# Sliding-window attention and a two-layer feed-forward in float32: value products by key block in array quarters, k and v in rings, whole scores in the opening, TensorE dummies and a new order

## The chip, the cores and the metric

The kernel runs on one core of one Trainium2 chip. The metric is the device time of one execution in microseconds (us); the median of the runs is given, and a profiled execution stands beside it.

## What is computed

Inputs are q, k and v of 8 batches, 8 heads, 576 positions and 64 columns, and the weights of a feed-forward network of 512 columns with 2048 hidden units. Positions see the 64 positions up to their own.

```
scores = q @ k.T / sqrt(64)                # where 0 <= i - j < 64, else -1e9
attn   = exp(scores - max) ; attn = attn / (sum + 1e-9)
x      = attn @ v, heads side by side       # 4608 x 512
h      = x @ w_in                           # 4608 x 2048
g      = max(h, 0) + alpha * min(h, 0)
out    = g @ w_out                          # 4608 x 512
```

The weights arrive as float64 bit patterns in int32 pairs and are made into floats on the chip.

## The kernel before, in words

The 4608 positions are 36 tiles of 128. A tile spans two query blocks of 64, each of which needs two key blocks of 64, so it needs three key blocks. The 8 heads are four pairs; two pairs lie above each other on the partitions (a "couple" of heads is the half of the partitions that a pair takes). For each tile t:

- `q_load`, `k_load` (three key blocks) and two `v_load` (two key blocks each) fetch into two buffers a name. Neighbouring tiles share a key block, which is fetched twice for k, and v is fetched twice over.
- `a_score` (line 433) writes the scores with products of 64x64 weights on 128 columns, in two PSUM banks, one for each half of the partitions. In the steady part both halves are written in one go, four quarters of the array side by side; in the opening tiles 0 to 2 (`WHOLE`) are too, tiles 3 to 8 one half at a time, with one bank each.
- `a_least` (444, VectorE) adds the mask and finds the maximum, `a_exp` (451, ACT) takes the exponential and its sum, `a_sum`, `a_inverse`, `a_scale` (462, 467, 473) divide.
- The weights of attention are turned: in the opening by TensorE (`a_turn`, 490) and a copy (`a_turned`, 495 or 497), later by VectorE's 32x32 transposes (`a_transpose`, 485).
- `a_value` (507) multiplies with v: 16 products with 128 rows (two key blocks) and 64 columns of weights, two halves of the array side by side, into one bank. `a_xh` (513, ACT) and `a_xl` (518, VectorE) split the result into a high and a low float32r part.

The feed-forward works on blocks of 2 or 3 tiles (`SIZES`), each in 16 cells of 128 hidden units. `m_hidden` (565) makes 12 products of high and low parts (high times high, low times high, high times low) into one of two PSUM buffers ("ph"); `m_slopes` (574, ACT), `m_larger` (580, VectorE), `m_high` (587, ACT) and `m_low` (594, POOL) make the activation and its two parts; `m_add` (608) makes three products for each tile into its output bank, two cells later (`LAG`).

float32 products are recorded twice each by the profile, float32r products once.

Weights come in 32 chunks (`raw`), and VectorE, ACT and POOL turn each into a high and a low part (lines 339 to 390: `two`, `man`, `exp`, `val`, then `win_h`, `win_l` or `wout_h`, `wout_l`). This and the attention of tiles 0 to 8 and the first three blocks of two tiles make the opening. Its order is written by a planner: `opening_graph` lists the operations with an engine, a cost and what they need; `list_schedule` walks through time and gives each engine, among what is ready and finds a buffer, the operation with the highest rank. The rank is the longest path to the end plus a number from `favour` (`TILE_FAVOUR`, `BLOCK_FAVOUR`, `KIND_FAVOUR`). PSUM has 8 banks in three pools: "po" 3, "psa" 3, "ph" 2. From tile 9 on, the order is written by hand: `eighth` cuts the attention of a tile into eight portions that are placed between cells; scores of tile t+1 and values of tile t-1 are in the last portion, next to each other.

Of the kernel before, what the change touches and what calls it, by code (L numbers as in the profile page):

```python
# [14 lines left out]
ALU = mybir.AluOpType  # L15
# [10 lines left out]
WHOLE = (0, 1, 2)  # L26
# [11 lines left out]
def opening_graph():  # L38
# [9 lines left out]
    def load(name, service, after=(), take=(), queue="SP"):  # L48
        op("i." + name, queue, 0.64, after, [take] * bool(take) + [("lane " + name, ["lane"])])
        op(name, "DMA", service, ["i." + name], free=["lane " + name])  # L50
# [6 lines left out]
    for t in range(EARLY + 1):  # L57
        done = [f"s.{t-2}.0", f"s.{t-2}.1"] if t > 1 else []
        load(f"q.{t}", 1.05, done, queue="ACT" if t == 0 else "SP")
        load(f"k.{t}", 1.6, done)  # L60
        for u in range(2):
            load(f"v.{t}.{u}", 1.05, [f"av.{t-2}"] if t > 1 else [])
    for c in range(2 * NCELL):
        load(f"raw.{c}", 2.0 if c % 2 else 2.2, take=(f"raw.{c}", ["raw"]))

    for t in attention:
        bank = ["po", "psa"] if t < 2 else ["psa"]
        score = [f"k.{t}", f"q.{t}"]
        score += ([f"s.{t-1}.0", f"s.{t-1}.1"] if t else []) + ([f"av.{t-2}"] if t > 1 else [])
        if t in WHOLE:  # L70
            op(f"s.{t}.0", "PE", 0.94, score, take=[(f"s.{t}.0", bank), (f"s.{t}.1", bank)])
            op(f"s.{t}.1", "PE", 0.0, [f"s.{t}.0"], done=0.0)
        for u in range(2):
            if t not in WHOLE:
                op(f"s.{t}.{u}", "PE", 0.87, score, take=(f"s.{t}.{u}", bank))
            for e in range(NH_PAIRS):
                g = u * NH_PAIRS + e
                op(f"le.{t}.{g}", "DVE", 0.21,
                   [f"s.{t}.{u}"] + ([f"tu.{t-2}.0", f"tu.{t-2}.1"] if t > 1 else []) + (["le.%d.0" % t] if g else []),
                   free=[f"s.{t}.{u}"] if e == NH_PAIRS - 1 else [], done=0.36)  # L80
                op(f"ex.{t}.{g}", "ACT", 0.39, [f"le.{t}.{g}"], done=0.6)
            op(f"sm.{t}.{u}", "ACT", 0.25, [f"ex.{t}.{u*NH_PAIRS+e}" for e in range(NH_PAIRS)], done=0.35)
# [3 lines left out]
            op(f"td.{t}.{u}", "ACT" if t > 1 else "DVE", 0.55 if t > 1 else 0.6,  # L86
               [f"tu.{t}.{u}"] + ([f"av.{t-2}"] if t > 1 else []), free=[f"tu.{t}.{u}"])
        op(f"av.{t}", "PE", 1.0, [f"td.{t}.0", f"td.{t}.1", f"v.{t}.0", f"v.{t}.1"]
           + ([f"h.{(t-RING)//2}.{last}"] if t >= RING else []), take=(f"av.{t}", bank))
        op(f"xh.{t}", "ACT", 0.5, [f"av.{t}"])  # L90
        op(f"xl.{t}", "DVE", 0.6, [f"xh.{t}"], free=[f"av.{t}"])

# [20 lines left out]
    for n in range(3):  # L113
        pair = [2 * n, 2 * n + 1]
        for f in range(NCELL):
            before = [f"h.{n}.{f-1}"] if f else [f"h.{n-2}.{last}"] if n > 1 else []
            op(f"h.{n}.{f}", "PE", 1.44, [f"lo.{2*f}"] + [f"xl.{t}" for t in pair] + before,
# [642 lines left out]
```

## Time and profile before

| | before |
|---|---|
| median of the runs | 934.62 us (934.35 to 934.86, 3 runs) |
| profiled execution | 934.54 us, its span 932.8 us |
| TensorE products busy | 912.3 us, 6601 records |
| VectorE, ACT, POOL busy | 438.0, 430.5, 348.1 us |
| moved by DMA | 69.78 MB, 75 GB/s on the mean; 254 GB/s in the first fortieth |
| loads, KB each, us to landing | q 256, 4.3; k 384, 4.7; v 256, 4.2; raw 512, 4.1 and 3.6 |

PE is TensorE's products, PEld its weight loads, DVE VectorE, ACT ScalarE, POOL GpSimd, SP the engine that issues most DMAs. A row of the windows has a stretch, its length, each engine's busy time with its count of instructions, the clock, the share of the DMA engines and what they moved. A row of the chain of waits has a start, a length, an engine, what it makes and its line. A row of the timeline has start, length, engine, line, operation, out<-in, shape and count, and in brackets the idle time before it with what ended it.

### The profile page before, as it was taken

To read this page: it belongs to the slowest core of one execution; us is meant where nothing else is said; L and a number is where in the kernel's file an instruction comes from. 1 tells how busy PE (TensorE), PEld (TensorE's weight loads), DVE (VectorE), ACT (ScalarE), POOL (GpSimd) and SP (SyncE) were. 2 spreads that over 40 slices of the span, in tenths; PEclk is the share of its full clock that TensorE was granted. 3 is DMA by queue.
4 is the path that set the end of the run, shared out by engine and by line. 5 is a ranking of instruction groups with operands and counts; after the bars stand their busy time and mean duration, and the time that the engine had idled before them with its cause. 6 is when DMAs were issued, how large, how long until landed. Compare 5 with 4: busy or idle time off the path is not lost.

```text
span 932.8 us, 17053 instructions
## 1 busy us (share of the span) xinstructions
PE 912.3 (98%) x6601; PEld 812.3 (87%) x6601; DVE 438.0 (47%) x1329; ACT 430.5 (46%) x1204; POOL 348.1 (37%) x330
## 2 busy tenths in 40 slices
PE   4899999999999999999999999999999999999998
PEld 3688889888988888888889889888888888889997
DVE  5798981224544444444444444444443443443111
ACT  5887884454444434434444444444443443432322
POOL 3889994224222233333222232332322222222221
PEclk9999999999999999999999999999999999999999
DMA  9775641111322112211122112222112212100000
GB/s 254 212 207 176 192 147 46 52 54 45 102 52 85 51 52 66 55 51 52 52 53 85 51 52 86 51 52 85 52 51 55 83 51 52 57 1 1 34 1 34
DMA packets 55216, 69.78 MB, mean 75 GB/s; under 512 B 3408, under 2 KB 48480, under 8 KB 55136
## 3 DMA queue, kind: packets, MB, share of 16 engines
q1 hardware_dynamic: 54832, 68.43, 26.0%
q8 instruction: 52, 0.85, 0.4%
q10 hardware_dynamic: 304, 0.27, 0.1%
q14 instruction: 28, 0.23, 0.1%
HBM read 59.25 MB, written 9.44 MB: 74 GB/s over the span
## 4 chain that ended last, share of the span: by engine, by line
PE 94%; DVE 2%; POOL 2%; ACT 1%; DMA 1%; issue 0%; POOLq 0%; DVEq 0%
PE h L565 43%; PE o L608 42%; PE s L433 4%; PE av L507 4%; PE t L490 1%; ACT w L451 1%; POOL val L375 1%; DMA q<-qT 1%; POOL w L473 0%; POOL gl L594 0%; POOL wout_l L390 0%; POOL win_l L390 0%; DVE exp L363 0%; DVE val L369 0%; DVE two L342 0%
## 5 line engine op out<-in xcount | busy, mean ns | idle before, releaser
L594 POOL TENSOR_TENSOR gl<-g,gh 128x384 fp32r<-128x384 f32 (+1 forms) x208 | 197.3, 948 | 548.9 <-ACT gh L587 543.3
L580 DVE SCALAR_TENSOR_TENSOR g<-h,s_sb,g 128x384 f32<-128x384 f32 (+1 forms) x208 | 122.0, 587 | 336.4 <-ACT g L574 333.6
L574 ACT ACTIVATE g<-h,sa_sb 128x384 f32<-128x384 f32 (+1 forms) x208 | 115.6, 556 | 262.7 <-PE h L565 258.4
L608 PE MATMUL o<-wout_h,gl 128*128 128x512 f32 x576 | 227.6, 395 | 1.2 <-POOL gl L594 1.2
L608 PE MATMUL o<-wout_l,gh 128*128 128x512 f32 x576 | 226.9, 394 | 0.0
L608 PE MATMUL o<-wout_h,gh 128*128 128x512 f32 x576 | 224.2, 389 | 0.0
L565 PE MATMUL h<-xh,win_h 128*128 128x384 f32 (+1 forms) x832 | 174.2, 331 | 0.4 <-DVE g L580 0.3
L565 PE MATMUL h<-xl,win_h 128*128 128x384 f32 (+1 forms) x832 | 168.8, 324 | 0.0
L565 PE MATMUL h<-xh,win_l 128*128 128x384 f32 (+1 forms) x832 | 167.8, 323 | 0.0
L587 ACT CAST gh<-g 128x384 fp32r<-128x384 f32 (+1 forms) x208 | 101.6, 489 | 124.4 <-DVE g L580 118.6
L565 PEld LDWEIGHTS h<-xh,win_h 128*128 128x128 f32 x832 | 141.3, 188 | 18.8 <-issue 1.2
L485 DVE STREAM_TRANSPOSE pt<-w 32x256 f32<-32x256 f32 x324 | 141.2, 436 | 5.5
L565 PEld LDWEIGHTS h<-xl,win_h 128*128 128x128 f32 x832 | 142.4, 188 | 0.1
L565 PEld LDWEIGHTS h<-xh,win_l 128*128 128x128 f32 x832 | 139.6, 188 | 0.0
L608 PEld LDWEIGHTS o<-wout_h,gh 128*128 128x128 f32 x576 | 108.1, 188 | 24.2
L451 ACT ACTIVATE w<-w,nm 128x128 f32<-128x128 f32 x288 | 113.1, 396 | 28.0 <-DVE nm L444 27.7
L608 PEld LDWEIGHTS o<-wout_h,gl 128*128 128x128 f32 x576 | 108.1, 188 | 18.5 <-POOL gl L594 1.8
L608 PEld LDWEIGHTS o<-wout_l,gh 128*128 128x128 f32 x576 | 108.3, 188 | 13.5
L444 DVE CUSTOM_DVE_ANT_0 w<-s,masks 128x128 f32<-128x128 f32 x288 | 71.1, 285 | 15.6 <-PE s L433 15.3
L473 POOL TENSOR_TENSOR w<-w,rc 128x1024 f32<-128x1024 f32 (+1 forms) x45 | 70.0, 1558 | 18.8 <-DVE rc L467 18.8
L518 DVE TENSOR_TENSOR xl<-av,xh 128x512 fp32r<-128x512 f32 x36 | 24.9, 691 | 99.6 <-ACT xh L513 99.5
L433 PEld LDWEIGHTS s<-k,q 64*64 64x64 f32 x1152 | 39.4, 142 | 24.0 <-PE o L608 9.6
(46 smaller groups left out, 535.1 us busy)
## 6 DMA issues: line engine op xcount, KB each, us to landing
v<-vN SPq DMA_DIRECT2D x72, 256.0 KB, 4.2
k<-kT SPq DMA_DIRECT2D x36, 384.0 KB, 4.7
out<-os SPq DMA_DIRECT2D x36, 256.0 KB, 2.3
q<-qT SPq DMA_DIRECT2D x35, 256.0 KB, 4.3
raw<-w_in SPq DMA_DIRECT2D x16, 512.0 KB, 4.1
raw<-w_out SPq DMA_DIRECT2D x16, 512.0 KB, 3.6
q<-qT ACTq DMA_DIRECT2D x1, 256.0 KB, 5.2
alpha_rows<-alpha ACTq DMA_DIRECT2D x1, 8.0 KB, 5.0
```

The lines of the kernel that those rows point to most:

```text
L433: nc.tensor.matmul(s[x][us, 2 * a + h], q[r, a, h, us], k[r, a, u:u + 2, h, :], start=True, stop=True)
L444: nc.vector.tensor_tensor_reduce(out=d["w"][:, g, :], in0=d["s"][u][:, e], in1=mask, op0=ALU.add, op1=ALU.min, scale=-SCALE, scalar=3.0e38 ...
L451: nc.scalar.activation(w, w, AF.Exp, scale=-1.0, bias=d["nm"][:, g:g + 1], accum_out=d["sm"][:, g:g + 1])
L473: nc.gpsimd.tensor_tensor(out=w, in0=w, in1=rc.unsqueeze(2).broadcast_to(list(w.shape)), op=ALU.mult)
L485: nc.vector.transpose(pt[ks, :, r], w[r, :, ks])
L507: nc.tensor.matmul(av[r, e, us], v[:, e, u, r], pt[:, g, us], start=True, stop=True)
L565: nc.tensor.matmul(ph[:, :nt], wt[:, c, fs], xt[:, c, xs], start=(k == 0), stop=(k == 3 * NP - 1))
L574: nc.scalar.activation(g, ph[:, :nt], AF.Copy, scale=sa_sb[:, f:f + 1])
L580: nc.vector.scalar_tensor_tensor(out=g, in0=ph[:, :nt], scalar=s_sb[:, f:f + 1], in1=g, op0=ALU.mult, op1=ALU.max)
L587: nc.scalar.copy(gh, gs[n, f])
L594: nc.gpsimd.tensor_tensor(out=gl, in0=g, in1=gh.bitcast(F32), op=ALU.subtract)
L608: nc.tensor.matmul(po[t], gt[:, ts], wt[:, f, :], start=(f == 0 and k == 0), stop=(f == NF - 1 and k == 2))
```

## The change

- **Values.** `a_value` takes each key block by itself: 32 products of 64x64 weights on 64 columns, four quarters of the array side by side, two of them (the index b) added up in PSUM. The two halves of the partitions go to two banks; outside the opening these are one "psa" and one "ph". High and low parts are then split by half: two `a_xh` and two `a_xl` for each tile, 256 columns each.
- **Rings.** k and v are const tiles of 7 key blocks (`KRING` = 3 tiles). Two tiles of three fetch only their two new key blocks; the third fetches three. v is one load for a tile.
- **Scores.** All tiles of the opening write both couples in one go. Tile 0 alone (`APART`) writes the two pair groups one after the other, and its q and k come in two loads each.
- **Layout.** The weights of attention lie as [pair group, key block, head, 64] so that the turned weights have each couple on its half of the partitions. `a_transpose` makes four transposes where it made three, two of them on half the columns; `a_scale` makes two calls of four heads in the steady part as well.
- **Dummies.** 60 products of the 128x128 identity with itself (`WARM`), at the lowest rank, in one "po" bank. The identity is now made before the masks.
- **First cells.** For the first three cells of each block (`FINE`) the three groups of products are operations of their own: high times high needs no low part. `m_add` starts with the high part.
- **Planner.** Other load costs, other favours with a third number for each kind, ties broken by index, and `MOVED`, a list of 13 copies given to VectorE (six `td`, seven `xh`); the other `td` go to ACT. The planner can also move `gl`, `pr`, `lo` and the sign of a chunk to VectorE; the list has none of these.

```diff
-WHOLE = (0, 1, 2)
+APART = (0,)
+WARM = 60
+FINE = 3
+KRING = 3
+MOVED = (
+    "td.0.0", "td.0.1", "td.4.0", "td.5.0", "td.5.1", "td.8.1", "xh.1.0", "xh.3.0", "xh.4.1", "xh.5.0",
+    "xh.5.1", "xh.6.0", "xh.7.0",
+)
...
+    for i in range(WARM):
+        op(f"wm.{i}", "PE", 1.2 if i == 0 else 0.25, [f"wm.{i-1}"] if i else [], take=("wm", ["po"]) if not i else (),
+           free=["wm"] if i == WARM - 1 else [])
...
+        values = ["po", "psa"] if t < 2 else ["psa", "ph"]
...
+    def k_load(t, a=None):
+        at = 2 * (t % KRING)
+        new = 1 if at else 0
+        part = slice(0, 2) if a is None else slice(a, a + 1)
+        from_ = kT[:, :, 2 * t + new:2 * t + 3].rearrange("(a x) d b h w -> (x d) a (b h w)", x=2)
+        nc.sync.dma_start(kring[:, part, at + new:at + 3].rearrange("p a b h w -> p a (b h w)"), from_[:, part])
+
+    def v_load(t):
+        at = 2 * (t % KRING)
+        new = 1 if at else 0
+        nc.sync.dma_start(vring[:, :, at + new:at + 3].rearrange("p a b d -> p a (b d)"),
+                          vN[:, :, 2 * t + new:2 * t + 3].rearrange("(a x) w b d -> (x w) a (b d)", x=2))
...
-        for e in range(NP):
+    def a_value(t, banks=("psa", "ph")):
+        pt, at = pts[t % 2], 2 * (t % KRING)
+        st[t]["av"] = av = [a_bank(f"av_{t}_{x}", from_) for x, from_ in enumerate(banks)]
+
+        for a in range(2):
             for u in range(2):
-                for h in range(2):
-                    r, us, g = slice(h * D, (h + 1) * D), slice(u * W, (u + 1) * W), e % 2 * NP + e // 2 * 2 + h
-                    nc.tensor.matmul(av[r, e, us], v[:, e, u, r], pt[:, g, us], start=True, stop=True)
+                for b in range(2):
+                    for h in range(2):
+                        for x in range(2):
+                            r, us, hs = slice(x * W, (x + 1) * W), slice(u * W, (u + 1) * W), slice(h * D, (h + 1) * D)
+                            nc.tensor.matmul(av[x][hs, a, us], vring[r, a, at + u + b, hs], pt[r, a, b, h, us],
+                                             start=b == 0, stop=b == 1)
...
-        for k, (gt, wt) in enumerate(((gl, wout_h), (gh, wout_l), (gh, wout_h))):
-            nc.tensor.matmul(po[t], gt[:, ts], wt[:, f, :],
+        for k in parts:
+            of_g, wt = (("gh", wout_h), ("gl", wout_h), ("gh", wout_l))[k]
+            nc.tensor.matmul(po[t], g[of_g][:, ts], wt[:, f, :],
                              start=(f == 0 and k == 0), stop=(f == NF - 1 and k == 2))
...
+    def warm(i):
+        if i == 0:
+            cv["warm"] = ps_o.tile([P, E], F32, tag="po", name="warm")
+        nc.tensor.matmul(cv["warm"][:, :P], ident, ident, start=True, stop=True)
```

More of the change, by code (lines that the diff above doesn't have):

```diff
@@ L58, in opening_graph @@
         done = [f"s.{t-2}.0", f"s.{t-2}.1"] if t > 1 else []
[L59 to L62, printed above, removed]
-    for c in range(2 * NCELL):
-        load(f"raw.{c}", 2.0 if c % 2 else 2.2, take=(f"raw.{c}", ["raw"]))
+        for a in range(2) if t in APART else ("",):
+            part = 0.5 if t in APART else 1.0
+            load(f"q.{t}" + f".{a}" * (a != ""), 0.8 * part, done, queue="ACT" if t == 0 else "SP")
+            load(f"k.{t}" + f".{a}" * (a != ""), (1.2 if t % KRING == 0 else 0.8) * part, done)
@@ L69, in opening_graph @@
[L69 to L72, printed above, removed]
-        for u in range(2):
[L74 to L77, printed above, removed]
+        before = ([f"s.{t-1}.0", f"s.{t-1}.1"] if t else []) + ([f"av.{t-2}"] if t > 1 else [])
@@ new lines, in opening_graph @@
+        for u in range(2):
+            loaded = [f"{x}.{t}.{u}" if t in APART else f"{x}.{t}" for x in "qk"]
+            banks = [(f"s.{t}.{x}" + ".1" * (u and t in APART), bank) for x in range(2)]
+            if t in APART:
+                op(f"s.{t}.{u}", "PE", 0.5, loaded + before + [f"s.{t}.0"] * u, take=banks)
+            elif u == 0:
+                op(f"s.{t}.0", "PE", 0.94, loaded + before, take=banks)
+            else:
+                op(f"s.{t}.1", "PE", 0.0, [f"s.{t}.0"], done=0.0)
@@ L280, in banded_attention_then_prelu_ffn @@
     ps_a = ctx.enter_context(tc.tile_pool(name="ps_a", bufs=3, space=PSUM))
+    ident = const.tile([P, P], F32, name="ident")
+    nc.gpsimd.memset(ident, 1.0)
+    nc.gpsimd.affine_select(out=ident, in_=ident, compare_op=ALU.is_equal, fill=0.0,
+                            base=0, pattern=[[-1, P]], channel_multiplier=1)
     masks = const.tile([P, 3, KW], F32, name="masks")
@@ L325, in banded_attention_then_prelu_ffn, with on, late_sign @@
     cv = {}
+    graph = opening_graph()
+    def on(name):
+        return {"POOL": nc.gpsimd, "DVE": nc.vector}[graph[name].engine if name in graph else "POOL"]
+    def late_sign(c):
+        return c % 2 == 1 and graph[f"lo.{c}"].engine == "DVE"
     def fetch(c):
@@ L346, in exponent @@
         two = cv[c]["two"]
-        nc.scalar.activation(two, two, AF.Relu, scale=8.0, bias=ebias if c % 2 else ebias20)
+        nc.scalar.activation(two, two, AF.Relu, scale=8.0, bias=ebias if c % 2 and not late_sign(c) else ebias20)
     def mask_mantissa(c):
@@ new lines, in of_x, with a_xh, a_xl @@
+    def of_x(t, of, x):
+        n, i = tiles[t]
+        return of.rearrange("p (a x) t -> p x a t", x=2)[:, x, :, (place[n] + i) * P:(place[n] + i + 1) * P]
+    def a_xh(t, x):
+        high, av = of_x(t, xh, x), st[t]["av"][x][:, :2]
+        if f"xh.{t}.{x}" in graph and graph[f"xh.{t}.{x}"].engine == "DVE":
+            nc.vector.tensor_copy(high, av)
+        else:
+            nc.scalar.copy(high, av)
+    def a_xl(t, x):
+        nc.vector.tensor_tensor(out=of_x(t, xl, x), in0=st[t]["av"][x][:, :2], in1=of_x(t, xh, x).bitcast(F32),
```

322 lines of the change are left out of this document (180 added, 142 removed).

## The prediction

> **What bounds the kernel now.** I read the page first, then the table of windows, then the chain of waits in three stretches, then single rows of the timeline.
>
> ```profile
> span 932.8 us, 17053 instructions
> PE 912.3 (98%) x6601; PEld 812.3 (87%) x6601; DVE 438.0 (47%) x1329; ACT 430.5 (46%) x1204; POOL 348.1 (37%) x330
> PE 94%; DVE 2%; POOL 2%; ACT 1%; DMA 1%; issue 0%; POOLq 0%; DVEq 0%
> ```
>
> TensorE is busy for 98% of the span and holds 94% of the chain that ended last. The other engines are below half on average, but the average hides the opening:
>
> ```profile
> core 0: us, PE busy (x) PEld busy (x) DVE busy (x) ACT busy (x) POOL busy (x), PEclk, DMA share, GB/s
> 0.00:10.00 10.00, 2.19 (x33) 1.76 (x33) 1.83 (x19) 2.36 (x6) 3.42 (x13) 1.00 0.87 214
> 10.00:20.00 10.00, 6.89 (x74) 5.45 (x75) 7.58 (x35) 7.93 (x32) 3.12 (x3) 1.00 1.10 293
> 20.00:30.00 10.00, 6.35 (x72) 4.63 (x70) 8.34 (x30) 7.05 (x27) 7.97 (x7) 1.00 0.96 267
> 30.00:40.00 10.00, 8.76 (x76) 7.42 (x74) 8.31 (x30) 8.71 (x29) 6.41 (x7) 1.00 0.70 202
> 60.00:80.00 20.00, 19.57 (x151) 16.89 (x150) 18.05 (x32) 15.40 (x33) 19.78 (x19) 1.00 0.52 157
> 100.00:120.00 20.00, 20.00 (x163) 17.51 (x163) 19.59 (x46) 17.34 (x45) 20.00 (x20) 1.00 0.60 191
> 200.00:900.00 700.00, 700.00 (x4944) 628.74 (x4943) 305.94 (x964) 287.75 (x823) 204.93 (x181) 1.00 0.20 55
> ```
>
> There are three stages. Until 30 us TensorE is busy for 2.19 + 6.89 + 6.35 = 15.4 us; half of the time it waits. From 60 us it is full, but up to 120 us (in these rows) so are POOL (19.78 and 20.00 of 20) and VectorE (18.05 and 19.59), which convert the weights. From 200 us TensorE alone is full. So work taken off TensorE after 60 us shortens the run directly, unless POOL holds it in the middle stage; before 33 us only the chain of waits counts.
>
> The chain of waits in the opening:
>
> ```profile
> 0.81 5.20 DMA q<-qT
> 6.06 2.05 PE s L433 x32
> 12.71 1.13 PE t L490 x4
> 14.70 1.10 PE t L490 x4
> 23.28 2.04 PE s L433 x30
> 28.76 1.55 PE av L507 x24
> 30.31 1.93 PE s L433 x22
> 89.56 1.02 PE s L433 x16
> ...
> 104.67 0.44 PE t L490 x4
> 110.79 1.02 PE s L433 x16
> 111.81 1.63 PE h L565 x12
> 114.81 1.44 PE h L565 x12
> ```
>
> and in the steady part:
>
> ```profile
> 610.11 1.03 PE s L433 x32
> 611.15 1.08 PE av L507 x32
> 612.23 2.28 PE h L565 x12
> 616.57 2.11 PE h L565 x12
> ```
>
> (Each float32 product stands twice in the records, so a tile's 16 score products are x32.) Two things are to be seen. All 32 records of a tile take 1.03 us where both couples run together; a half with one couple, 16 records, takes 1.02, as long for half the work. And the same pieces cost double at the start: 2.05 against 1.03 for scores, 1.13 against 0.44 for four transposes. TensorE runs at half speed until past 30 us, although the clock column prints 1.00 there. The first cell of the feed-forward part starts right behind:
>
> ```profile
> 32.86 0.74 PE L565 MATMUL h<-xh,win_h 128*128 128x256 f32 x4
> ```
>
> **The change part by part.** The profiled execution took 934.54 us for its span of 932.8, beside a median of 934.62 for the runs, so I sum against 934.5.
>
> **Scores of both couples at once.** Tiles 3 to 8 scored in halves. A half costs 1.02 and slows its neighbour by the switch of tile shape (1.63 against 1.44 for h: 0.2), 1.22 in all; two cost 2.44. A whole tile costs 1.03 + 0.2 = 1.23. That saves 1.2 per tile; tiles 4 to 8 lie where TensorE is nearly full, so 5 x 1.2 = **-6.0**. The price is that two PSUM banks are taken at one moment; a wait for that would show in front of the scores.
>
> **Value products in quarters.** 32 products of 64x64 on 64 columns replace 16 of 128x64 on 64 columns: 64 records instead of 32, but four side by side where there were two, so again 16 steps. The rows for one step:
>
> ```profile
> 586.92 1.10 PE L433 MATMUL s<-k,q 64*64 64x128 f32 x32
> 587.95 1.01 PEld L507 LDWEIGHTS av<-pt,v 128*64 128x64 f32 x32 [0.17 <-issue]
> 587.95 1.15 PE L507 MATMUL av<-pt,v 128*64 128x64 f32 x32
> 610.04 0.34 PE L433 MATMUL s<-k,q 64*64 64x128 f32 x4
> L433 PE MATMUL s<-k,q x1152: 269/269/473, 6.1 to 808.4; 64*64 64x128 f32 x192
> L507 PE MATMUL av<-pt,v x1152: 222/222/370, 15.7 to 853.7; 128*64 128x64 f32 x192
> issue: 5.7, 29
> ```
>
> Less the last product's own 0.22, 1.15 leaves 0.93 for 15 pair steps: 0.062 each for 64 columns. Scores leave 1.10 - 0.27 = 0.83 for 7 steps of four, 0.119 for 128 columns. Twice the columns, nearly twice the time, with two or four side by side: the step follows the columns. The first four scores of a tile lie within 0.34 us, where one alone lasts 0.27 or more, so issuing four takes hundredths. I therefore keep 0.062 and count **0**, with 0.119 (the score step) as the upper bound and nothing below zero, since the columns stay.
>
> **The border between scores and values.** Both now use the same quarters. The value weights waited 0.17 in the row above; in all 5.7 us over 29 waits, 0.20 each ("issue" on that line). If the quarters stay as they are, this wait goes. The bounds are 0 and 0.20; I take 0.13, because the next step would have taken 0.062 anyway. In the steady part 25 tiles (values 9 to 33) have scores directly ahead: 25 x 0.13 = **-3.3**.
>
> **The head: dummies, split loads, finer first cells.** The half-speed pieces on the chain shrink if the clock is up: scores 2.05 to 1.03 and 2.04 to 1.03, transposes 2.23 to 0.88, values and scores 1.55 and 1.93 to 0.8 and 1.03, together 5.0 less. But between them stands VectorE's queue (8.34 of 10 us busy from 20 to 30), so a part is only handed to it: I take half, -2.5. Tile 0's loads come in halves, so the first scores need half the bytes of the 5.20 us load; I take -0.5, because the dummies are in front of them: ten queued products of 128 columns at half speed (two records of 0.22 each) are 4.4 us, which begin only when POOL has made the identity that they multiply. The first three cells no longer wait for low parts, and k and v fetch a third less while the DMA is full (0.87 to 1.10 of share until 30 us): -1.5 together. Dummies that land behind real work: 60 x 2 x 0.119 = 14 us at full speed, and TensorE stands idle for 14.6 of the first 30, so nearly all fits; I add +0.8. Sum: **-3.7**. The bounds are -9 (VectorE's idle time from 10 to 40 us, 30 - 7.58 - 8.34 - 8.31 = 5.8, and 3 for an earlier start) and +7 (half of the dummies in the way, nothing gained). The sizes -0.5, -1.5 and +0.8 are choices inside these bounds.
>
> The Trainium skill, page "TensorE: Matmul & The Clock Gate", section "What's actually happening", says that the clock doubles after some 3.4 us of sustained matmuls and falls back after a window without any. The trace agrees in part: with 6.89 busy of 10 it stayed slow, and it rose only after the unbroken run from 28.76 on. By that rule the dummies raise it at 5 to 9 us.
>
> **At no cost.**
>
> ```profile
> L580 DVE SCALAR_TENSOR_TENSOR g<-h,s_sb,g 128x384 f32<-128x384 f32 (+1 forms) x208 | 122.0, 587 | 336.4 <-ACT g L574 333.6
> L574 ACT ACTIVATE g<-h,sa_sb 128x384 f32<-128x384 f32 (+1 forms) x208 | 115.6, 556 | 262.7 <-PE h L565 258.4
> L485 DVE STREAM_TRANSPOSE pt<-w 32x256 f32<-32x256 f32 x324 | 141.2, 436 | 5.5
> L518 DVE TENSOR_TENSOR xl<-av,xh 128x512 fp32r<-128x512 f32 x36 | 24.9, 691 | 99.6 <-ACT xh L513 99.5
> ```
>
> Each eviction of values (0.69 on VectorE) becomes two of half the columns, and a tile's 12 VectorE transposes of 0.44 become 16, half of them of half length: under 1 us per tile on engines that are busy for 306 and 288 of 700 us. POOL scales the same elements in two halves. One value bank now comes from the pair of buffers that h turns over. The next h then needs the previous cell's buffer back; between lie nine o products (in the chain from 612.23 + 2.28 to 616.57, 2.06), scores and values, 2.06 + 1.03 + 1.08 = 4.2 us, while slope and maximum take 0.56 + 0.59. Three microseconds of cover remain; gone, it would cost its excess 27 times. On SP one v load for two waits at the same place, ahead of the same stores.
>
> Sum: -6.0 + 0 - 3.3 - 3.7 = -13.0, so **921.5 us**. All lower bounds together give 934.5 - 6.0 - 5.0 - 9 = 914.5; with the head at 0 it is 925, and 927 if half of the border's gain is missing too.
>
> **Rivals.** *The middle stage is POOL's.* From 60 to 120 us POOL is as full as TensorE. If cells come no faster than POOL makes weights, what TensorE saves there turns into waiting. Against it: TensorE shows no idle time at all from 100 to 120, and the third block's cells can fill in. It would lose half of the -6.0 and most of the -3.7: 934.5 - 3.0 - 3.3 - 0.7 = 927.5, or up to 933 if the new order also starves TensorE.
>
> *Quarters cost more (the other side).* If four products cannot be fed in 0.062, the step becomes that of the scores: 16 x (0.119 - 0.062) = 0.91 per tile, over the 32 tiles from tile 4 on 29 us: 934.5 - 13 + 29 = 950.5. It decides from a step of 0.062 + 13/(32 x 16) = 0.087 upward. For it: no row shows four products, with their four weight loads, sustained in 0.062; scores sustain four in 0.119. Against it: scores and values keep the same time per column, and the 0.34 above shows the burst. The same page of the Trainium skill, section "Wait — 56ns, not 53.3ns?", gives a floor of about 25 ns between starts however short the product; four would need 0.10 us, an estimate of +20 us for the same tiles and so 941, slower. The rows of scores average 0.119 / 4 = 0.030 and those of values 0.031, which does not refute it; the burst of four does, if the floor were for each start.
>
> *The clock does not rise,* or the dummies are late. The head's gain goes and they cost a few us: 934.5 - 9.3 + 2 = 927.
>
> **How the numbers follow.** The forecast 0.55; middle stage or clock 0.22 (927 to 933.5, of which 0.04 lies within 0.2%); better than 914, if VectorE regains all its idle time in the head, 0.07; quarters dearer 0.13 (above 934.5 to 951); other losses, such as a wait for banks in every tile, 0.03. Less than 0.2%, 1.9 us, cannot be told from no change. Faster by more: 0.55 + 0.22 - 0.04 + 0.07, and 0.01 for dearer quarters that the rest still covers, 0.81; same 0.05; slower 0.14. The range 913 to 934 leaves out the dear quarters, the other losses and a few hundredths below.
>
> **What would show it.** Right: scores only as x32 from tile 1 on; in the steady part the values as x64 in about 0.95 to 1.0 us, their weights without the 0.17 in front; scores of 1.03 and transposes of 0.44 before 20 us; the first h near 28 us instead of 33; TensorE full from 60 us on. Wrong: values at 1.5 us or more per tile; idle time on TensorE in front of o or h between 60 and 140 us with POOL as releaser; scores of 2.05 us still there; a wait of h for VectorE's value evictions; a steady period that is not shorter.

## The result, and the profile after

| | before | after |
|---|---|---|
| median of the runs | 934.62 us (933.98 to 934.86, 5 runs) | 927.6 us (925.92 to 930.8, 5 runs) |
| ratio to before, with its 95% interval | | 0.9932 [0.9909, 0.9954] |
| profiled execution, its span | 934.54, 932.8 us | 925.92, 924.2 us |
| moved by DMA | 69.78 MB | 58.95 MB |

The kernel is faster by 7.0 us, little more than half of the forecast, 13.0 less or 921.5 us; the range, 913 to 934, holds the result. The profiled execution is the fastest of its five, 1.7 us below their median, so its profile shows more gain than the median has. A second series of the unaltered kernel gave 927.25 us (927.0 to 928.8, 5 runs), ratio 0.9921 [0.9908, 0.9935]. I measure the experiments on the changed kernel against 927.4, the middle of the two medians; a ratio is always to the kernel before, run beside them.

The page of the changed kernel, the lines that were shown of before:

```profile
span 924.2 us, 19726 instructions
PE 912.4 (99%) x7873; PEld 818.5 (89%) x7873; DVE 461.5 (50%) x1482; ACT 427.4 (46%) x1231; POOL 352.3 (38%) x357
PE 90%; DVE 4%; POOL 2%; DMA 2%; ACT 1%; issue 1%; DVEq 0%; ACTq 0%; POOLq 0%
```

TensorE's busy time is the same, 912.4 us against 912.3, but dummies are in it now. Its table of windows:

```profile
0.00:10.00 10.00, 8.25 (x81) 7.31 (x85) 2.66 (x25) 3.81 (x15) 3.38 (x13) 1.00 0.81 249
10.00:20.00 10.00, 10.00 (x164) 9.64 (x154) 9.14 (x32) 8.19 (x32) 4.55 (x5) 1.00 0.72 241
20.00:30.00 10.00, 9.97 (x187) 9.18 (x185) 9.48 (x46) 9.06 (x31) 8.94 (x8) 1.00 0.90 292
30.00:40.00 10.00, 7.89 (x124) 5.84 (x124) 9.09 (x21) 9.20 (x31) 8.36 (x9) 1.00 0.56 169
33.00:64.00 31.00, 25.62 (x310) 19.43 (x308) 29.13 (x84) 28.68 (x89) 30.43 (x29) 1.00 0.67 209
100.00:120.00 20.00, 20.00 (x122) 17.59 (x121) 17.83 (x32) 14.10 (x30) 19.77 (x20) 1.00 0.53 159
200.00:900.00 700.00, 700.00 (x5798) 633.13 (x5797) 325.07 (x1092) 287.83 (x843) 210.00 (x209) 1.00 0.14 44
```

and before's row for 33 to 64 us:

```profile
33.00:64.00 31.00, 29.03 (x260) 24.08 (x261) 28.62 (x85) 27.76 (x84) 25.11 (x24) 1.00 0.73 205
```

The columns are TensorE's products, its weight loads, VectorE, ACT and POOL. Until 30 us TensorE looks nearly full, because dummies fill it. Between 33 and 64 us, where no dummy is left, it now idles 31 - 25.62 = 5.4 us, where it idled 2.0 before, while VectorE, ACT and POOL are busy for 29.13, 28.68 and 30.43 of 31.

The chain of waits in the opening and in the steady part (start, length, engine, what, line):

```profile
1.75 4.62 PE warm L764 x20
6.37 0.60 PE s L509 x16
9.65 1.03 PE s L509 x32
12.22 0.45 PE t L575 x4
25.64 4.68 DMA raw<-w_out
38.67 5.17 DMA raw<-w_in
...
602.65 1.03 PE s L509 x32
603.68 0.93 PE av L595 x64
604.61 2.31 PE h L657 x12
608.98 2.11 PE h L657 x12
```

Scores at 9.65 us take 1.03 and transposes 0.45: the clock rose, as forecast. The values are x64 in 0.93 us where they were x32 in 1.08. The timeline shows their weights with no idle time before them (before: 0.17), and the first two cells of the feed-forward part:

```profile
22.29 0.74 PE L657 MATMUL h<-xh,win_h 128*128 128x256 f32 x4
28.76 0.72 PE L657 MATMUL h<-xh,win_h 128*128 128x256 f32 x4
...
603.40 1.08 PEld L595 LDWEIGHTS av<-pt,v 64*64 64x64 f32 x64
```

The span divides well at the scores of tile 9, where the order written by hand begins. The row of each kernel, before and after:

```profile
200.78 1.10 PE L433 MATMUL s<-k,q 64*64 64x128 f32 x32
```

```profile
195.34 1.10 PE L509 MATMUL s<-k,q 64*64 64x128 f32 x32
```

The opening is 5.4 us shorter (forecast: 6.0 + 3.7 = 9.7). From there to the end it is 932.8 - 200.78 = 732.0 before and 924.2 - 195.34 = 728.9 after, 3.1 us shorter (forecast: 3.3). So the steady part did what was expected, and the missing time is in the opening. The profile of the second series (span 927.1) shows that the scatter of the changed kernel lies there too: it has the same 728.9 us from tile 9's scores on, but they start 2.9 us later, only 2.6 us ahead of before.

```profile
198.22 1.10 PE L509 MATMUL s<-k,q 64*64 64x128 f32 x32
```

At 33 us the changed kernel is far ahead: 24 products of h (`m_hidden`) have begun where before had 1, and 5 of o (`m_add`) where it had none. By 64 us 97 and 40 have begun, against 92 and 36. Most of the lead was given back in the stretch in which TensorE now idles.

### The profile page after: what moved, and what is told of

Its sections match the earlier page's. It is cut to its first block, busy times and chain, and to the rows that moved or that the text cites. A ratio compares the mean times of both kernels' runs of the same rounds, so it can differ in the third digit from the quotient of the medians.

```text
span 924.2 us, 19726 instructions
## 1 busy us (share of the span) xinstructions
PE 912.4 (99%) x7873; PEld 818.5 (89%) x7873; DVE 461.5 (50%) x1482; ACT 427.4 (46%) x1231; POOL 352.3 (38%) x357
## 2 busy tenths in 40 slices
DMA packets 45468, 58.95 MB, mean 64 GB/s; under 512 B 2864, under 2 KB 38720, under 8 KB 45376
## 3 DMA queue, kind: packets, MB, share of 16 engines
q8 instruction: 62, 1.02, 0.5%
## 4 chain that ended last, share of the span: by engine, by line
PE 90%; DVE 4%; POOL 2%; DMA 2%; ACT 1%; issue 1%; DVEq 0%; ACTq 0%; POOLq 0%
PE h L657 42%; PE o L699 40%; PE s L509 4%; PE av L595 3%; DMA raw<-w_in 1%; DMA raw<-w_out 1%; POOL val L434 1%; PE warm L764 1%; DVE man L408 1%; DVE two L398 1%; DVE exp L421 1%; POOL gl L684 1%; DVE val L428 1%; PE t L575 0%; POOL win_l L456 0%
## 5 line engine op out<-in xcount | busy, mean ns | idle before, releaser
L699 PE MATMUL o<-wout_l,gh 128*128 128x512 f32 x576 | 223.9, 390 | 0.0
L566 DVE STREAM_TRANSPOSE pt<-w 32x256 f32<-32x256 f32 x216 | 94.1, 436 | 3.1
L550 POOL TENSOR_TENSOR w<-w,rc 128x512 f32<-128x512 f32 x72 | 73.8, 1041 | 17.2 <-DVE rc L546 16.5
L610 DVE TENSOR_TENSOR xl<-av,xh 128x256 fp32r<-128x256 f32 x72 | 27.1, 419 | 85.3 <-ACT xh L607 85.3
L569 DVE STREAM_TRANSPOSE pt<-w 32x128 f32<-32x128 f32 x216 | 65.5, 303 | 4.0
```

The costliest lines, as they stand in the source:

```text
L550: on(f"sc.{t}.{u}").tensor_tensor(out=w, in0=w, in1=rc.unsqueeze(1).unsqueeze(3).broadcast_to(list(w.shape)), op=ALU.mult)
L566: nc.vector.transpose(to.rearrange("p a b h q -> p (a b h) q"), w[:, x, j].rearrange("p a b h k -> p (a b h) k"))
L569: nc.vector.transpose(to[:, :, j ^ 1], w[:, x, j, :, j ^ 1])
L699: nc.tensor.matmul(po[t], g[of_g][:, ts], wt[:, f, :], start=(f == 0 and k == 0), stop=(f == NF - 1 and k == 2))
```

## The experiments

The question is what holds TensorE between 33 and 64 us, and what the dummies and the new order are worth. My theory after the result: VectorE's queue, which converts the weights in order, sets the pace there, so a faster TensorE only arrives earlier at a wait. The rivals: POOL or ACT sets it; the weight loads do, which stand in the chain with 4.68 and 5.17 us; or a PSUM bank does, since the exponents of a chunk (`two`) lie in one of the two buffers of h until VectorE's sign step (`exp`) has read them. What TensorE waits for from 33 to 64 us in the changed kernel (total, times, longest) names POOL, ACT and VectorE, the last with the step that frees the bank:

```profile
PE h L657 <- POOL win_l L456: 1.5, 1, 1.5
PE av L595 <- ACT pt L583: 1.3, 2, 0.9
PE h L657 <- DVE exp L421: 1.3, 1, 1.3
```

**The dummies taken out.** All but the first are left out, and the order stays.

```diff
-        nc.tensor.matmul(cv["warm"][:, :P], ident, ident, start=True, stop=True)
+        if i == 0:
+            nc.tensor.matmul(cv["warm"][:, :P], ident, ident, start=True, stop=True)
```

> The changed kernel in its own order, with 59 of the 60 dummies left out. Theory A (from 33 to 64 us VectorE, ACT and POOL set the pace, so a lead of TensorE at 33 us is given back): scores take 2.05 us again until about 30 us and the first cell comes later, but the total loses 0 to 2.5 us against the changed kernel's 927.6, so 927 to 930. Rival B (the clock is worth the 5 us of the chain, and something else ate the gain): 931 to 934. Rival C (the dummies stand in the way of real work): faster than 927. If the changed kernel's scatter of 5 us comes from a clock that falls back after the dummies, it is gone here (all runs within 1 us) or shows as a lower clock in all of them.

Measured: 925.6 us (925.37 to 926.49, 4 runs), ratio 0.9903 [0.9888, 0.9918], some 1.8 us less than with them, though the intervals overlap (0.9909 to 0.9918). My theory had 927 to 930; the time is that of the rival by which the dummies stand in the way. Timeline and windows of its profiled run:

```profile
4.02 1.13 PE L509 MATMUL s<-k,q 64*64 64x128 f32 x16 [1.47 <-DMA q<-qT]
8.37 1.99 PE L509 MATMUL s<-k,q 64*64 64x128 f32 x32 [0.84 <-DVE s_sb L750]
```

```profile
16.00:20.00 4.00, 3.15 (x48) 2.44 (x52) 4.00 (x8) 2.73 (x7) 1.96 (x2) 0.50 0.16 48
```

The scores take 1.99 us again, and the clock reads 0.50 in that row: the clock is down, and nothing is lost. The first h starts at 22.1 us (22.3 with the dummies), and at 33 us both kernels have begun 24 products of h. So the dummies, with the higher clock that they bring to the opening, are worth nothing in this kernel. The clock alone has no price from this run, because the dummies also delay the start: without them the first scores start at 4.02 us, when the half loads have landed, with them at 6.30, behind 4.62 us of dummies. Of these 2.3 us 1.2 are left at the scores of tile 1 (8.37 against 9.58) and 0.2 at those of tile 4 (36.34 against 36.57).

**The dummies alone, in the kernel before.** 60 of them in before's planner, with the identity made first.

```diff
+WARM = 60
+    for i in range(WARM):
+        op(f"wm.{i}", "PE", 1.2 if i == 0 else 0.25, ...
```

> The kernel before, with the 60 dummies put into its planner's list at the lowest rank and the identity made first; nothing else. Theory A: the early scores take 1.03 and transposes 0.44, but the total gains at most 1.5 us: 933 to 935. Rival B: the chain of 5 us shows in full or by half, 929.5 to 932. Rival C: slower than 935.

Measured: 940.73 us (940.02 to 941.32), 1.0063 [1.0048, 1.0078], slower than 935 as rival C had it, but not shown to be for its reason. The planner answered them with another order: the first h starts at 42.0 us (before: 32.9), and TensorE waits 5.8 us for POOL's scaled weights in front of transposes. This does not isolate the clock in before's own order; that stays open.

**Whole scores alone, in the kernel before.**

```diff
-WHOLE = (0, 1, 2)
+WHOLE = tuple(range(9))
```

> The kernel before, with all tiles of the opening scored in both couples at once (its planner then puts them into its own order). By the prediction's term 5 tiles x 1.2 = 6.0: 928.6. Theory A: only the halves behind 64 us count, 3.5 tiles x 1.2 = 4.2, so 930 to 931, with more idle time of TensorE between 33 and 64 us. If two banks at once cost waits: 933 or more, with VectorE in front of the scores or the turns.

Measured: 938.63 us (938.08 to 939.2), 1.0041 [1.0026, 1.0056]: 4 us slower where the term was to bring 6.0. What TensorE waits for from 64 to 205 us (total, times, longest):

```profile
PE o L608 <- POOL gl L594: 2.5, 3, 1.2
PE h L565 <- DVE exp L363: 1.9, 3, 1.5
PE t L490 <- POOL w L473: 1.2, 1, 1.2
```

Before has one such wait, of 0.3 us. The time is that of the last case (933 or more), but most of the waiting stands in front of o and h, not of the scores. In the order that before's planner makes here, the saving is lost in waits.

**The changed kernel with before's rank numbers.**

```diff
-TILE_FAVOUR = [554, 313, 218, ...]
+TILE_FAVOUR = [305, -52, 78, 372, ...]
```

(`BLOCK_FAVOUR` and the pairs of `KIND_FAVOUR` likewise.)

> The changed kernel with the rank numbers of the kernel before (the third number of each kind 0), so its planner makes another order; everything else as changed. The whole scores alone made the kernel before slower by 4 us, with 7 us of waits of TensorE between 64 and 205 us. Theory E (what the opening gains is gained by the new order; two banks at once cost waits in an order that is not made for them): 930 to 938 and over 5 us of TensorE's idle time behind 64 us. Rival: the gain is in the parts themselves, 926 to 929.

Measured: 944.68 us (944.39 to 946.2), 1.0111 [1.0097, 1.0125], 17 us more than with the new numbers and beyond the 930 to 938 that I expected. From 64 to 214 us TensorE waits for:

```profile
PE t L574 <- POOL w L549: 3.6, 3, 2.1
PE s L508 <- DVE nm L522: 1.6, 1, 1.6
PE h L656 <- DVE g L669: 1.6, 4, 0.6
```

The new numbers are no side matter: without them the other parts together make the kernel 10 us slower than before.

**The weight loads.** Chunks from the third on are converted from the data of the first two.

```diff
+        if c < 2:
+            nc.sync.dma_start(raw, ...)
+            cv["raw", c] = raw
+        raw = cv["raw", c % 2]
```

> The changed kernel without the weight loads from the third chunk on: every later chunk is converted from the first two chunks' data, so no conversion waits for a load; the results are of other weights. Rival D (the weight loads, 4.3 to 5.2 us each on the chain, which the planner now prices lower, took the head's lead): TensorE's idle time from 33 to 64 us falls from 5.4 to under 2.5 and the time to 921 to 924. Theory A: conversions are limited by their engines, 925.5 to 928 and at least 4 us of idle time left.

Measured: 923.97 us (923.73 to 924.7), 0.9886 [0.987, 0.9903]. The DMA share from 33 to 64 us falls from 0.67 to 0.19, and TensorE still idles 4.7 us there. The time is the rival's (921 to 924), the idle time is my theory's (4 us or more). So the loads cost 3.4 us in the whole run, clear of the scatter, but waiting for them is not most of TensorE's idle time there.

**Each engine relieved in turn.** Steps of the conversion are left out for every chunk but the first: POOL's product; VectorE's mask of the exponent and its sign step together with ACT's copy between them; ACT's copy alone; VectorE's sign step alone.

```diff
+        if c == 0:
             on(f"pr.{c}").tensor_tensor(out=d["val"], ..., op=ALU.mult)
```

> The changed kernel without POOL's product of weight value and exponent for all chunks but the first (the results are of other weights): 1.3 us less of POOL for each of 31 chunks, the order kept. Theory A1 (POOL sets the pace from 33 to 64 us): TensorE's idle time there falls from 5.4 to under 2 and the time by 3 to 5 us, to 921 to 924. A2 (VectorE sets the pace): idle time stays at 4 or more, and the time at 925 to 927.

```diff
+        if c:
+            return
```

(in the functions of `two`, of ACT's copy and of `exp`)

> The changed kernel without the exponent's two VectorE operations and its ACT operation for all chunks but the first; POOL's product is kept, with the value itself as its second operand (the results are of other weights): 1.2 us less of VectorE and 0.55 less of ACT for each of 31 chunks, the order kept. A2 (VectorE sets the pace from 33 to 64 us): idle time there under 2.5, time 920 to 923. A1 (POOL sets it): idle time of 4 or more, 924.5 to 927. If all three are level, each of the two kernels gains only 1 to 2 us.

(the same in one function alone, ACT's copy, then `exp`)

> The changed kernel without the exponent's ACT operation for all chunks but the first (other weights): 0.55 us less of ACT for each of 31 chunks, VectorE and POOL as they were. Without this one, VectorE's two and POOL's product the time fell to 921.2; without POOL's product alone it stayed at 927.5. A2v (VectorE's queue sets the pace): 925.5 to 927.5. A2a (ACT's queue): 921.5 to 924.

> The changed kernel without the VectorE operation that joins sign and exponent, for all chunks but the first; POOL's product takes the value itself as its second operand (other weights): 0.6 us less of VectorE for each of 31 chunks, ACT and POOL as they were. A2v: about half of the 6 us that two operations of VectorE gave, 923.5 to 925. A2a: 926 to 928.

| left out | median (range) | ratio | against 927.4 |
|---|---|---|---|
| POOL's product | 927.51 (926.41 to 928.0) | 0.9922 [0.9909, 0.9936] | 0.1 |
| ACT's copy | 926.82 (924.68 to 927.57) | 0.9909 [0.9894, 0.9923] | -0.6 |
| VectorE's sign step | 924.69 (923.71 to 925.94) | 0.989 [0.9877, 0.9904] | -2.7 |
| VectorE's mask and sign step, ACT's copy | 921.18 (921.08 to 921.71) | 0.9858 [0.9844, 0.9871] | -6.2 |

Their windows from 33 to 64 us, in the order POOL, ACT, sign step, all three:

```profile
33.00:64.00 31.00, 25.41 (x304) 20.83 (x303) 27.81 (x81) 27.01 (x86) 17.89 (x18) 0.89 0.64 198
```

```profile
33.00:64.00 31.00, 25.94 (x316) 20.47 (x316) 29.92 (x85) 24.35 (x78) 30.88 (x30) 1.00 0.67 209
```

```profile
33.00:64.00 31.00, 26.52 (x320) 21.00 (x321) 24.74 (x75) 27.98 (x86) 29.11 (x30) 1.00 0.70 211
```

```profile
33.00:64.00 31.00, 27.66 (x333) 23.15 (x334) 20.54 (x69) 25.49 (x81) 30.45 (x31) 1.00 0.70 225
```

Only the last two times are clear of the changed kernel's intervals. In the first row POOL (fifth column) has 12.5 us less than in the changed kernel, and TensorE (first) does no more, also beside the second series with the same clock of 0.89 (25.75); in the last, POOL is as full as ever, VectorE (third) has 8.6 us less, and TensorE does 2.0 more, though it still idles 3.3 where I expected under 2.5. The end moves with the conversion: POOL has made the low part of the last chunk by 134.3 us in the changed kernel, by 134.4, 132.9, 132.3 and 128.6 in these four, and by 142.2 in the kernel before. So the fullest row, POOL's, is not the one that counts. But leaving out the sign step also takes a link out of each chunk's chain and releases the bank earlier, and leaving out the mask never takes it: these runs do not tell VectorE's time from the bank.

**Time or bank.** Two kernels free the bank and leave VectorE its work: the sign step reads the raw data in place of the bank, in the second one without ACT's copy as well.

```diff
-        ..., in0=d["high"], scalar=-2**31, in1=d["two"],
+        ..., in0=d["high"], scalar=-2**31, in1=d["high"] if c else d["two"],
```

> The changed kernel, except that VectorE's sign step of every chunk but the first takes its second operand from the raw data and not from the PSUM bank that ACT's exponent copy writes. VectorE, ACT and POOL do as much as before; only the bank, one of the two that the products of h turn over, is free when ACT is done, and the sign step waits for nothing but the data. So the weights that come out are others. Theory VectorE's time: leaving out the sign step gained 2.7 us because VectorE had 0.6 us less for each chunk; here it has as much, so no gain: 927.4, within 1.2. Rival, the bank: h waits 1.3 us for the sign step between 33 and 64 us because that step holds the bank, and the 2.7 us came from its release; then 924.5 to 925.5.

> As the kernel with the earlier release, and ACT's exponent copy left out too (every chunk but the first): the bank is free as soon as VectorE's own mask has written it, half a microsecond after it was taken. VectorE still does all three steps. Leaving out mask, copy and sign had gained 6.2 us. Theory VectorE's time: nothing but what leaving out ACT's copy gave, -0.6: 926.8, within 1.2. Rival, the bank: most of the 6.2 comes without any less work on VectorE: 922 to 923.5.

Measured: 936.29 us (935.89 to 936.99, 11 runs), 1.0019 [1.001, 1.0028], and 936.83 us (936.41 to 938.13, 9 runs), 1.0026 [1.0017, 1.0036]. Neither theory had this: 9 us slower. The groups of the first show why (the last columns are busy time and the mean of one):

```profile
L421 DVE SCALAR_TENSOR_TENSOR exp<-raw 128x512 int32<-128x512 int32 x31 | 36.5, 1178 | 2.2 <-POOL val L434 2.2
L434 POOL TENSOR_TENSOR val<-val,exp 128x512 f32<-128x512 f32 x32 | 46.8, 1464 | 5.1 <-DVE val L428 3.3 <-DVE rc L546 1.6
```

With both operands from SBUF the sign step takes 1178 ns, where it took 680, and POOL's product 1464, where it took 1292. VectorE and POOL get in each other's way (the last section shows how), and VectorE has 475.6 us instead of 461.5. The runs do not price the bank, but show what longer steps of VectorE and POOL cost; and with a longer step in both, freeing the bank sooner still (the second) brings nothing.

So the sign step was given the mantissa's bank to read, which it holds in any case, again without ACT's copy:

```diff
+        ..., in1=d["man"].bitcast(I32) if c and "man" in d else d["two"],
```

(all 31 chunks behind the first read the mantissa's bank)

> The changed kernel, except that for every chunk but the first ACT's exponent copy is left out and VectorE's sign step takes its second operand from the mantissa's PSUM bank, which it holds until the join in any case. The two runs that took it from the raw data had doubled the sign step (0.68 to 1.2 us), so they could not price the bank; here it is a PSUM operand again and should last 0.68. The weights that come out are others. VectorE does all it did; the bank that h turns over is held only for VectorE's own mask, some 0.6 us. Halving VectorE's two steps had given 926.1, about half of what leaving out the sign step gave (924.7). If VectorE's time is what counts: what leaving out ACT's copy alone gave, 926.8, within 1.2. If the bank, or the wait of the sign step for ACT, holds the stretch: most of the 6.2 of leaving out mask, copy and sign, 922 to 924. A value between, 924 to 925.5, says that both count.

Measured: 925.85 us (925.05 to 927.98, 4 runs), 0.991 [0.9893, 0.9926]; the sign step lasts 680 ns again. That is 1.0 less than without ACT's copy alone, within the scatter of both, and far from 921.18: that the bank is held for long is not what gave the 6.2. Two limits remain. The sign step and ACT's step on the mantissa now wait for each other (0.8 and 2.3 us in the whole run), and the mask still takes a bank, which it did not in the run of 921.18. But in the changed kernel the mask hardly ever waits, for a bank or for anything else; VectorE stands idle in front of all 32 of them for 0.7 us:

```profile
L398 DVE TENSOR_SCALAR two<-raw 128x512 int32<-128x512 int32 x32 | 22.0, 688 | 0.7 <-DMA raw<-w_in 0.3
```

The counterpart keeps the bank and halves VectorE's work: the sign step and the join (`val`) on 256 of 512 columns, from the third chunk on.

```diff
+        w = E if c < 2 else E // 2
-        ..., out=exp, in0=d["high"], ..., in1=d["two"],
+        ..., out=exp[:, :w], in0=d["high"][:, :w], ..., in1=d["two"][:, :w],
```

> The changed kernel, except that for every chunk but the first two VectorE's sign step and its join of the mantissa work on half of the columns, into two kept buffers each, so the other half of the weights is stale. VectorE has some 30 x 2 x 0.29 = 17 us less work in all, as much as without the sign step; the bank is held only 0.3 us shorter and every step still waits for what it waited for. Theory VectorE's time: the same gain as without the sign step, -2.7: 924.7, within 1. Rival, the bank: 927.0, within 0.8.

Measured: 926.08 us (925.96 to 926.82, 4 runs), 0.991 [0.9897, 0.9924]: 1.3 less, between the two numbers, and the intervals overlap. So my theory stands only in part. Of the three engines only VectorE's conversion moves the end by more than the scatter when it is relieved: 2.7 us, and 6.2 with the mask and ACT's copy; how long the bank is held does not explain it. But its time in sum is not the measure: 13.3 us of VectorE (461.5 - 448.2 in the profiles) gave 1.3 as two halves, and 16.8 (461.5 - 444.7) gave 2.7 as one whole step, which also takes a link out of each chunk's chain. How much of the gain is the shorter chain and how much the time stays open.

**More dummies.** 120 of them; then 120 with none before tile 0's scores. Both keep the planner's numbers.

```diff
-WARM = 60
+WARM = 120
```

> The changed kernel with 120 dummies instead of 60: the planner has them left for TensorE's idle time behind 28 us. In one profile of the unaltered kernel the clock fell to half near 43 us and the span was 927.1, in the other it did not and the span was 924.2. If that is the scatter: no clock below 1.0, runs within 1 us, median 925 to 926. If dummies stand in the way: 927 to 930.

```diff
-[f"wm.{i-1}"] if i else []
+[f"wm.{i-1}"] if i else ["s.0.1"]
```

(with `WARM = 120`)

> The same 120 dummies, but none before tile 0's scores. The kernel without dummies began those at 4.0 us instead of 6.3, yet had lost that lead at 64 us. If both matter, the start and a clock that does not fall: 923.5 to 925. Theory A2v (VectorE's queue sets the pace, whatever TensorE's clock): 925 to 926, as without dummies (925.6).

Measured: 934.67 us (933.64 to 936.13, 11 runs), 0.9999 [0.999, 1.0008], and 937.83 us (936.95 to 938.73, 7 runs), 1.0032 [1.0021, 1.0043]. The first one from 33 to 64 us, all work and then the dummies alone (products, weight loads):

```profile
33.00:64.00 31.00, 31.00 (x394) 28.89 (x395) 28.36 (x83) 27.83 (x87) 28.96 (x27) 1.00 0.63 192
33.00:64.00 31.00, 11.70 (x78) 10.91 (x78) 1.00 0.63 192
```

The idle time is gone and the clock is up in every run, and the kernel is 7 us slower (10 in the second run), where I expected 927 to 930 at the worst. 39 dummies (x78) stand in that stretch; the 31st product of o starts at 76.0 us instead of 60.9. The dummies take TensorE's time and hold one of the three output banks; I take no shares for bank and time from this; the runs do not divide them.

**VectorE relieved in a kernel that leaves no computation out.** The 13 copies that `MOVED` gives to VectorE go to ACT, without dummies.

```diff
-        if graph[f"td.{t}.{u}"].engine == "DVE":
-            nc.vector.tensor_copy(pt, tp)
+        nc.scalar.copy(pt, tp)
```

(and the same for `xh`)

> The changed kernel without 59 of the dummies (925.6 on the median) and with all copies of turned weights and high parts on ACT, in the planner's same order: some 6 us of VectorE's work, about 2 of them before 64 us, go to ACT. If VectorE's queue sets the pace from 33 to 64 us and ACT has room (without 0.55 us of its work for each chunk nothing was gained): 923.5 to 925. If ACT takes its place: 925.5 to 928.

Measured: 925.37 us (924.48 to 927.12, 4 runs), 0.9901 [0.9886, 0.9916], beside 925.6 without dummies alone: no gain that can be told. From 33 to 64 us VectorE has 27.50 of 31, 0.9 less than without dummies alone, and 16.8 us of the sign step in the whole run were worth 2.7: too little to show. This run neither bears the theory out nor refutes it.

**The border undone in the steady part.** Without dummies, the scores of tile t+1 go two eighths ahead of the values of tile t-1.

```diff
-        elif k == 7:
             a_score(t + 1)
+        elif k == 7:
```

(the neighbouring step stays in the eighth before)

> The changed kernel without 59 of the dummies, and in the steady part the scores two eighths ahead of the values instead of directly before them, cells between. If the third term of the prediction is right (a border between 64x64 scores and 64x64 values costs nothing, one to or from 128x128 products 0.1 to 0.2 each): values take 1.09 instead of 0.93, and one more neighbour is slowed by 0.2, over 25 tiles 7 to 10 us: 932.5 to 936. If the value steps themselves are faster in quarters, values stay at 0.93 and the time below 931.

Measured: 933.79 us (932.83 to 935.67, 10 runs), 0.9993 [0.9984, 1.0003], 8.2 us more than the same kernel with scores and values together. Its chain:

```profile
602.67 1.03 PE s L509 x32
603.71 2.29 PE h L657 x12
608.05 1.09 PE av L595 x64
609.15 2.31 PE h L657 x12
613.51 2.11 PE h L657 x12
```

Alone, the values take 1.09 instead of 0.93, and a second h is slowed, 2.29 against 2.11. That is 0.16 + 0.18 = 0.34 for a tile, 8.5 us over 25 tiles, beside 8.2 measured.

**The unaltered kernel again.**

> The changed kernel once more, unaltered, beside the others on one chip. Its five runs lay between 925.9 and 930.8, those without dummies between 925.4 and 926.5. If the dummies make the scatter and cost 2 us on the median, it comes again: median 927 to 928.5 and a spread over 2 us. If the difference was the other chip: median 925 to 926 and a spread near 1 us.

Measured as told above: 927.25 us, with a spread of 1.8 us, so the 2 us beside the kernel without dummies come again. The clock goes with its scatter: the row of 42 to 48 us here, and in the first profile:

```profile
42.00:48.00 6.00, 4.72 (x67) 3.47 (x69) 5.97 (x20) 5.67 (x18) 5.41 (x6) 0.59 0.56 177
```

```profile
42.00:48.00 6.00, 4.64 (x86) 3.46 (x85) 5.83 (x14) 5.97 (x19) 5.98 (x6) 1.00 0.54 166
```

In the slower of the two profiled runs (span 927.1 against 924.2) the clock was down to half from 43.0 to 49.9 us, and tile 5's scores start at 51.4 us instead of 48.4. The ten runs of the unaltered kernel agree: the four whose mean granted clock is 0.994 to 0.996 took 927.67 to 930.8 us, the six at 1.00 took 925.92 to 927.6. So a clock that falls behind 33 us does go with a longer run, while the higher clock ahead of 33 us, dummies included, brought nothing. Why the kernel without dummies, whose clock falls as well (0.66 from 40 to 50 us), still takes less time stays open.

## Why the prediction was partly right

**The border: right.** -3.3 was forecast, the steady part is 3.1 shorter, and undoing it costs 0.16 on the values where I took 0.13 from a wait of 0.17 to 0.20. "The quarters stay as they are" is the reason, and the run with scores and values apart bears it out. The Trainium skill, page "TensorEngine Tiling (Array Packing)", section "Key Properties", says that a change of tiling mode drains TensorE and a change of tile alone does not; the 0.93 against 1.09 agrees.

**Quarters at no cost: right.** The values take 1.09 alone, as 1.08 before, and the rival *quarters cost more* (0.087 or more for a step, 950.5 us) is refuted by the 0.93 of the border. The 25 ns floor of the Trainium skill's page "TensorE: Matmul & The Clock Gate", section "Wait — 56ns, not 53.3ns?", does not hold for quarters: 64 records in 0.93 us are 14.5 ns each on the mean, and as many weight loads beside them.

**The failed step: the head.** "I take half, -2.5", for pieces on the chain that shrink with the clock. The pieces did shrink (2.05 to 1.03, 1.10 to 0.45), and yet the time came out no longer without the dummies, at half the clock. I had named VectorE's queue, busy 8.34 of 10 us, as what stands between the pieces, and still let half of their gain through. With the delay of the first scores that the dummies bring, none of it came through; what the clock alone would give was not measured. What the runs show in its place: the end follows the conversion of the weights, VectorE's steps above all (6.2 us without three steps, two of them VectorE's) and the loads beside them (3.4), and a TensorE that is ahead at 33 us waits for it ahead of 64. The other parts of the term, as far as the runs size them: the half loads let the first scores start 2.0 us sooner (4.02 against 6.06; I took 0.5), but only without dummies. The dummies in the way, taken at +0.8, cost 1.8 by the medians, the gain of their clock already set off. The first cells came earlier than forecast (22.3 us, "near 28"), and most of that lead was given back; as it is there without dummies too (22.1), the clock did not make it. The finer first cells and the smaller loads, taken at -1.5, were not measured apart. Forecast for all the head: -3.7. What is left, from the opening's -5.4 and the next term, is about -1.4 in the profiled execution; the median is 1.7 us longer, so on the median nothing is left.

**Whole scores: right in kind, too large by a third.** I counted five tiles of 1.2 us "where TensorE is nearly full". Behind 64 us, where it is full, lay only seven halves, 3.5 tiles: 112 records at 1.02 for 16. There are three whole tiles there now, 96 records at 1.03 for 32, so 7.14 us became 3.09, or 4.05 less, of which 0.5 is the half tile that moved ahead of 64 us. The rest lies ahead of 64 us, where TensorE idles more than before, so that what it saves becomes waiting. And the term rests on the new rank numbers, which I did not price: in the order of before's planner whole scores cost 4 us.

**The rivals.** *The middle stage is POOL's*: its number, 927.5, came true by luck, not by its mechanism. From 64 to 200 us TensorE idles 0.25 us, and leaving out POOL's product changes nothing. The waiting lies before 64 us, and of the three engines VectorE's steps are worth most. *The clock does not rise*: it rose, at 6.2 us in the first profile, and its number, 927, came near for another reason.

The point "TensorE full from 60 us" held (idle 0.25 us from 64 to 200, 0.29 before); "the first h near 28 us" was too late by six.

**A version that beats both** is the changed kernel without its dummies, 925.6 us, by 9.4 against the kernel before beside it (934.98) and, less surely, by 1.8 against the change.

## What to carry to other kernels

Before you book a gain in a stretch where several engines are nearly full, relieve each in turn to find whose steps move the end: the fullest row (POOL here, 30.43 of 31) need not be the one, and what TensorE saved there turned into waiting. Count what dummies delay as well as the clock that they raise: here the first scores waited behind them, and the kernel without them was no slower. In the steady part put products of one tile shape next to each other: each change of shape costs 0.16 to 0.20 us here, and between other operands of the same shape none is seen.

## What the runs showed of the hardware

**VectorE and POOL.** VectorE's sign step of 0.68 us became one of 1.18 on the mean, 1.78 at the most, when its second operand came from SBUF and not from PSUM, and POOL's conversion steps beside it grew by 0.1 to 0.2. The timeline of that run shows the two side by side:

```profile
40.23 1.29 POOL L434 TENSOR_TENSOR val<-val,exp 128x512 f32<-128x512 f32 x1
40.85 1.21 DVE L421 SCALAR_TENSOR_TENSOR exp<-raw 128x512 int32<-128x512 int32 x1
41.47 1.72 POOL L456 TENSOR_TENSOR win_l<-val,win_h 128x512 fp32r<-128x512 f32 x1
```

VectorE's step ends 0.54 us after POOL's first, less than its own 0.68, and POOL's next takes 1.72, where 1.30 is its mean in the changed kernel. It is no accident of this one: 28 of the 31 steps end 0.55 us after the POOL instruction that they found running, whether that had 0.14 or 1.23 us left; the other three found none, or one with under 0.1 left, and took 0.68 to 0.69. The Trainium skill, page "SBUF — State Buffer", section "Terms", says that VectorE and GpSimd take turns at a shared pair of ports, held for a whole instruction. The trace agrees, but for the first 0.13 us or so of the step, which run beside POOL's.

**Quarters.** Four 64x64 quarters sustain one record each 14.5 ns with as many weight loads; no row of the kernel before showed this for longer than a burst.

**The clock.** The column prints 1.00 ahead of the first change on record, even where products run at half speed: the row of 0 to 10 us of the run without dummies has 1.00 while its scores take 1.99 us instead of 1.03. In the traces of all the runs the stretches between two changes of the clock last 3.41 us or a multiple of it (3.41, 6.83, 10.24, 37.55). Where these steps fall differs from run to run. Counted in such steps, the clock fell 14 times ahead of the end, each time behind a step in which TensorE was busy for 1.00 to 1.77 us; with 1.86 or more it never fell, and three times it held with 1.63 to 1.78. It rose behind steps of 2.91 us or more, though twice it stayed down with 3.01 and 3.04. The prediction's words for the fall, "after a window without any" matmuls, do not fit these runs: about half a step was enough. In the second series the idle stretch near 40 us filled one step (1.12 us busy up to 43.0, then half the clock); in the first profile it was split over two (2.12 and 2.55), and the clock stayed up.
